# A retention kernel with its MLP: q only cast, the decay multiplied into the retention's result, and the work of all engines in another order

## The chip, the cores and the metric

One core of a Trainium2 chip runs the kernel. It has five engines with queues of their own: TensorE (PE, with PEld for its weight loads), VectorE (DVE), ScalarE (ACT), GpSimd (POOL) and SyncE (SP). Each engine takes its instructions in the order of the program and waits on semaphores where it needs another's result. Data move between the memory (HBM) and the core by DMAs that POOL, SP or ACT issue. The metric is the time of one execution in microseconds on the device; lower is better.

## The reference

Eight batches of eight heads, 576 positions, 64 wide; then a two-layer MLP over 4608 tokens:

```python
scores = scale * np.matmul(q, k.transpose(0, 1, 3, 2))
gamma = 1.0 - 2.0 ** (-5.0 - np.arange(H, dtype=np.float32))
rel = pos[:, None] - pos[None, :]
Dmat = np.where(rel >= 0, gamma[:, None, None] ** rel[None, :, :], 0.0)
attn_out = np.matmul(scores * Dmat[None, :, :, :], v)
x = np.ascontiguousarray(attn_out.transpose(0, 2, 1, 3)).reshape(B * S, H * D)
h = x @ w_in
return np.maximum(0.01 * h, h) @ w_out
```

The weight of a pair of positions is gamma to the power of their distance, so it splits into a factor of the later position (q's) and one of the earlier (v's).

## The kernel before

**Blocks.** The 4608 tokens are 36 blocks (`u`) of 128, each of two chunks of 64. A batch has nine chunks. Four blocks are a group `g` of 512 tokens, and there are nine groups. A position's decay is taken relative to the middle of a stretch of four chunks (256 positions), so that a table with one row for each position in the stretch serves all blocks.

**One block of retention.** `ld` loads q, k and v (0, 1, 2) as float32. `ck` casts k to float16. `cq` multiplies q with its decay and the scale and writes float16, `cv` does so for v; on DVE each is one multiplication with a broadcast table, on ACT eight small ones (`scaled`, L373). k and q are transposed, in blocks 0 to 7 on PE (`tp`, L411, with copies out of PSUM by `yt`, L418), later by a DMA of SP (`tr`, L397). `sa` makes the scores (L445), `mk` applies the causal mask (DVE, L460), `sb` makes the chunk's state (L454), `st` adds it to the running state (DVE, L485 to L491; at a stretch's end in two steps, through `stmp`, with gamma to the 256th), `sx` casts the state (L503, L506). `oa` makes the output from v and the masked scores and from q and the state (L542); from block 4 on it is parted into `ca` (scores of this block and the part of the output that crosses chunks) and `ow`. `x` (L591) casts the output from PSUM into the group's `xT`, float16, on ACT or DVE.

**The MLP.** Groups 0 and 1 run layer 1 as plain matmuls (`h`, L640, and the leaky ReLU `l`, L647). The other groups run it with seven products instead of eight (`a`, L833), and layer 2 does so for all groups (`b`, L911), with sums of weights and operands made by DVE (`ws`, `wm`, `xs`, `m`) and additions of the products (L857, L947). w_in comes in four quarters (`wi0` to `wi3`, L612), w_out in four (`wo`, L621), cast to float16 by POOL's DMAs.

**What sets the order.** `ORDER` is a list of job names, issued in that order: each engine's queue is the list with the other engines' jobs left out. `@n` picks a PSUM bank, and `+13@3` stands for 13 matmuls on a tile of zeros (`filler`, L977). `ENGINE` says which engine makes a cast or a copy. Pools have few buffers: a load for block `u + 4` waits until block `u`'s cast has read its buffer.

Of the kernel before, what the change touches and what calls it, by code (L numbers as in the profile page):

```python
# [33 lines left out]
class Plan:  # L34
# [52 lines left out]
    for eng, names in {  # L87
        "DVE": """
            ck0 cq0 sx0.0 yt0.0 cq1 sx0.1 cv1 cq2 sx1.0 yt2.1 ck3 cq3 yt3.1 cv3 sx2.1 yt3.0 cq4 cv4 x3 ck5 cq5
            cv5 yt5.1 cq6 sx5 cv6 cq7 ck7 cv7 yt7.0 b0.cA cv8 ck10 sx8.0 cv9 cq9 cq11 cq12 cv10 b1.cA cv13 ck15  # L90
            cv14 cq14 cv15 cq15 sx13.1 sx14 cq16 cv16 cv17 cq17 cq18 a2.3.k5 sx17.0 cv18 sx18 cq19 a3.1.u2 x17
            cv20 ck21 cq21 sx19 a3.2.k5 cq22 cv22 sx20 ck23 cv23 cq23 x20 cv24 cq25 sx23 a4.2.cA cv25 a4.2.u2
            cq26 cq27 cv27 sx25 a5.0.u2 a5.0.k5 cq28 cq29 cv29 ck30 cq30 cv30 ck31 cv31 cq32 sx30 cq33 ck33
            a6.0.cA cv33 cv34 ck34 cq35 cq34 a6.2.cA b5.u2 cv35 a6.3.u2 x32 a7.0.cA x33 a7.0.k5 b5.21 a7.1.cA
            b6.11 b6.u2 a7.3.cA a7.3.u2 a8.0.k5 b7.k5 a8.2.u2 a8.2.k5 b7.21 a8.3.u2 b8.21
        """,
        "ACT": """
            cv0 yt0.1 x0 ck1 ck2 yt1.1 yt1.0 cv2 yt2.0 x1 sx1.1 sx2.0 x2 sx3.0 ck4 sx3.1 yt4.1 yt4.0 ck6 sx4.1
            x4 yt5.0 x5 yt6.0 yt6.1 sx6 yt7.1 sx7 x7 x6 ck8 b0.11 cq8 ck9 b0.u2 cq10 b0.k5 cv11 ck12 sx9 x8 ck11
            cv12 sx10 cq13 b0.21 x9 ck13 sx11 b1.11 sx12 x10 b1.u2 x11 ck14 a2.0.cA b1.k5 a2.0.u2 a2.0.k5 x12  # L100
            a2.1.cA a2.1.u2 x13 a2.1.k5 ck16 ck17 sx15 a2.2.cA a2.2.u2 b1.21 a2.2.k5 sx16 x14 a2.3.cA x15
            a2.3.u2 ck18 b2.cA a3.0.cA b2.11 a3.0.u2 a3.0.k5 a3.1.cA cv19 b2.u2 x16 a3.1.k5 ck19 b2.k5 a3.2.cA
            ck20 cq20 a3.2.u2 cv21 b2.21 ck22 x18 a3.3.cA a3.3.u2 a3.3.k5 x19 b3.cA a4.0.cA b3.11 sx21 ck24
            a4.0.u2 a4.0.k5 cq24 a4.1.cA a4.1.u2 sx22.1 a4.1.k5 x21 b3.u2 ck25 b3.k5 ck26 sx24 a4.2.k5 x22 cv26
            a4.3.cA x23 a4.3.u2 a4.3.k5 ck27 b3.21 a5.0.cA b4.cA ck28 cv28 sx26.0 b4.11 x24 ck29 a5.1.cA a5.1.u2
            a5.1.k5 x25 sx27 sx28 b4.u2 a5.2.cA x26 sx29 b4.k5 a5.2.u2 a5.2.k5 x27 a5.3.cA ck32 a5.3.u2 cv32
            a5.3.k5 cq31 b4.21 x28 x29 sx31.1 a6.0.u2 a6.0.k5 sx32 b5.cA a6.1.cA b5.11 a6.1.u2 x30 a6.1.k5 x31
            a6.2.u2 a6.2.k5 sx33 b5.k5 ck35 a6.3.cA a6.3.k5 sx34 sx35.0 a7.0.u2 b6.cA a7.1.u2 a7.1.k5 a7.2.cA
            a7.2.u2 b6.k5 a7.2.k5 x34 x35 a7.3.k5 a8.0.cA b6.21 a8.0.u2 b7.cA b7.11 a8.1.cA b7.u2 a8.1.k5
            a8.1.u2 a8.2.cA a8.3.cA a8.3.k5 b8.cA b8.u2 b8.k5 b8.11x so8.11x b8.11y  # L110
# [11 lines left out]
    l0.4.256 tp4.0@2 x3 tp5.0@1 yt4.0 st3.1s ld6.1 h0.11.0@0 sx3.1 yt5.0 ld6.2 h0.9.0@2 yt4.1 ck5 cv4 ld7.0
    h0.10.0@1 l0.9.0 tp5.1@3 ld7.2 l0.10.0 ca4 sb4 h0.4.384@2 mk4 ld7.1 cv5 h0.8.0@1 l0.4.384 st4.1 ld8.2 yt5.1 ow4
    sb5 x4 h0.15.0@2 st5.0 sx4.1 st5.1 l0.11.0 h0.14.0@3 sx5 ld8.1 ca5 l0.14.0 cq6 l0.8.0 ld9.2 ws3.1 h0.13.0@0 mk5
    ld9.1 h0.0.128@3 l0.13.0 cv6 wo2 h0.0.384@1 l0.0.128 ld10.2 l0.15.0 tp6.0@0 h0.0.256@3 ck6 yt6.0 ld10.1 tp6.1@2
    l0.0.384 ow5 sb6 wo0 x5 h0.12.0@0 st6.0s yt6.1 ld8.0 h1.0.0@1 cv7 l0.0.256 cq7 ld9.0 h1.2.0@2 l1.0.0 ck7 st6.1
# [88 lines left out]
def kernel(  # L215
# [148 lines left out]
    def casts(u):  # L364
# [5 lines left out]
        def ck():  # L370
            copies[ke](out=by_half(t[:, 1]), in_=in_halves(t32[u, 1][:]))
# [680 lines left out]
```

## Time and profile before

| what | before |
|---|---|
| median of 3 runs (lowest, highest) | 279.20 us (279.14, 279.57) |
| the profiled execution: its time | 279.54 us |
| its span, first to last instruction | 277.7 us |
| PE busy | 268.1 us, 97% |
| PE's weight loads busy | 224.4 us, 81% |
| DVE busy | 229.8 us, 83% |
| ACT busy | 206.7 us, 74% |
| POOL busy | 72.4 us, 26% |
| HBM read, written | 36.81 MB, 9.44 MB |

Busy time is the time in which at least one instruction of the engine runs; matmuls overlap each other, and their ends are modelled. The profile gives for a group of instructions the number, the busy time, the mean duration of one, and the idle time ahead of them with what ended most of it. A timeline row has the start, the duration, engine, line, operation and the tiles (out `<-` in), how many were merged (`xN`), and idle time in brackets.

### The profile page before, as it was taken

What the parts mean: (1) busy time and instruction counts of PE and PEld (TensorE: products, weight loads), DVE (VectorE), ACT (ScalarE), POOL (GpSimd) and SP (SyncE); (2) the same over time, 40 slices, a digit from 0 to 9 for tenths busy, and PEclk for the clock granted to TensorE, in tenths of its full rate; (3) what the DMA queues carried; (4) which work ended last, traced back from release to release, by engine and by line L of the source; (5) the groups of instructions that cost most, each with busy time, mean ns of one, the idle gap of its engine ahead of it and who ended that gap; (6) DMA issues with size and microseconds to landing.
All of it is one profiled execution on the core that took longest, in us unless ns stands there. A gap on an engine that the chain in (4) does not pass through costs nothing.

```text
span 277.7 us, 10117 instructions
## 1 busy us (share of the span) xinstructions
PE 268.1 (97%) x4337; PEld 224.4 (81%) x4337; DVE 229.8 (83%) x431; ACT 206.7 (74%) x459; POOL 72.4 (26%) x92
## 2 busy tenths in 40 slices
...
GB/s 219 224 240 238 293 287 269 277 216 177 208 256 220 220 295 227 173 236 230 257 222 255 183 228 183 170 247 219 20 139 74 44 2 2 153 0 0 78 97 132
DMA packets 94364, 50.04 MB, mean 180 GB/s; under 512 B 83312, under 2 KB 88560, under 8 KB 94320
## 3 DMA queue, kind: packets, MB, share of 16 engines
...
q8 instruction: 34, 0.56, 0.8%
q10 hardware_dynamic: 432, 0.24, 0.3%
q14 instruction: 10, 0.08, 0.1%
HBM read 36.81 MB, written 9.44 MB: 167 GB/s over the span
## 4 chain that ended last, share of the span: by engine, by line
PE 91%; DMA 5%; POOL 1%; ACT 1%; issue 1%; DVE 1%; POOLq 0%
PE acc L911 39%; PE acc L833 32%; PE acc L640 10%; DMA t<-in_k_dram 5%; PE ot L542 5%; PE sc L454 2%; PE sc L445 2%; PE sc L911 1%; POOL t L346 1%; PE acc L411 1%; DVE s L487 0%; POOL w_in L612 0%; ACT st L503 0%; DVE qk L375 0%; DVE s L460 0%
## 5 line engine op out<-in xcount | busy, mean ns | idle before, releaser
L911 PEld LDWEIGHTS <-gt 128*128 128x128 f16 x720 | 69.8, 98 | 8.4
L346 POOL DMA_DIRECT2D t<-in_v_dram x40 | 34.2, 857 | 100.5 <-DVE v L375 64.0
L911 PE MATMUL acc<-w_out,gt 128*128 128x256 f16 x416 | 51.5, 273 | 0.0
L833 PEld LDWEIGHTS <-w_in 128*128 128x128 f16 x448 | 42.4, 98 | 5.6
L853 ACT ACTIVATE gt<-acc 128x512 f16<-128x512 f32 x56 | 33.4, 599 | 16.6 <-PE acc L833 16.4
L861 ACT ACTIVATE gt<-sum 128x512 f16<-128x512 f32 x56 | 34.8, 633 | 4.7 <-DVE sum L857 4.7
L911 PE MATMUL acc<-w_mix,gt 128*128 128x256 f16 x288 | 36.2, 273 | 0.0
L833 PEld LDWEIGHTS <-w_sum 128*128 128x128 f16 x336 | 32.2, 98 | 4.1
L833 PE MATMUL acc<-xs,w_sum 128*128 128x256 f16 x224 | 33.6, 273 | 0.0
L833 PE MATMUL acc<-xT,w_in 128*128 128x256 f16 x224 | 33.5, 273 | 0.0
L833 PE MATMUL acc<-xs,w_in 128*128 128x256 f16 x224 | 33.4, 273 | 0.0
...
L640 PE MATMUL acc<-xT,w_in 128*128 128x256 f16 (+2 forms) x272 | 30.8, 266 | 0.7 <-ACT qkT L418 0.4
L911 PEld LDWEIGHTS <-mix 128*128 128x128 f16 x288 | 28.1, 98 | 3.3
L460 DVE TENSOR_TENSOR s<-sc,cs 128x512 f16<-128x512 f32 x36 | 24.6, 684 | 4.4 <-PE sc L445 2.3
L640 PEld LDWEIGHTS <-w_in 128*128 128x128 f16 x272 | 22.0, 98 | 5.8 <-issue 0.9
L857 DVE TENSOR_TENSOR sum<-acc,k 128x512 f32<-128x512 f32 x28 | 19.2, 686 | 7.9 <-PE acc L833 5.7
L647 ACT ACTIVATE gt<-acc 128x512 f16<-128x512 f32 x32 | 18.2, 601 | 6.3 <-PE acc L640 6.2
L786 ACT COPY k<-acc 128x512 f32<-128x512 f32 x29 | 17.0, 588 | 7.5 <-PE acc L833 3.7
L375 DVE TENSOR_TENSOR qk<-t,cs 128x512 f16<-128x512 f32 x30 | 20.5, 684 | 2.3 <-DMA t<-in_q_dram 2.3
L591 ACT CAST xT<-ot 128x512 f16<-128x512 f32 x31 | 18.2, 588 | 4.6 <-PE ot L542 4.6
L381 ACT ACTIVATE v<-t,cs 128x64 f16<-128x64 f32 x72 | 18.3, 343 | 4.1 <-DMA t<-in_v_dram 3.4
...
## 6 DMA issues: line engine op xcount, KB each, us to landing
...
```

Of the source, the lines that this page charges most:

```text
L346: engine[eng].dma_start(out=t[CH * j : CH * j + rows], in_=(q, k, v)[x][b, :, CH * w : CH * w + rows, :].rearrange("h t d -> t h d"),)
L375: engine[e].tensor_tensor(out=view[0](out), in0=view[1](t32[u, 2 * x][:]), in1=view[1](decay(u, x)), op=MUL)
L381: nc.scalar.mul(out=out[:, at(h), :], in_=t32[u, 2 * x][:, h, :], mul=tab_sb[:, w, x, h : h + 1])
L460: landed[u] = nc.vector.tensor_tensor(out=s[:], in0=sc[:, :, 0], in1=mask_sb.unsqueeze(1).unsqueeze(1).to_broadcast([P, 2, NP, CH]), op=MUL,)
L591: moved[u] = copies[xe](out=x_of(u).rearrange("q c (j t) -> q j c t", j=2), in_=at)
L640: nc.tensor.matmul(out=a[:, n, :], lhsT=w_in16[:, c, (f0 + n) * P : (f0 + n + 1) * P], rhs=x[:, c, t0 : t0 + nt], start=(n == 0 and c == 0 ...
L647: nc.scalar.activation(out=y[:, f0 : f0 + nf, t0 : t0 + nt], in_=a[:], func=mybir.ActivationFunctionType.Lrelu)
L833: nc.tensor.matmul(out=r[:, f, :], lhsT=w[:, c, (2 * n + f) * P : (2 * n + f + 1) * P], rhs=rhs[:, c, :], start=fresh and c == 0 and f == ...
L853: w = op(what, "ACT", lambda: nc.scalar.activation(out=to(), in_=r[:], func=lr), after, [y], [r])
L857: what, "DVE", lambda: nc.vector.tensor_tensor(out=s[:], in0=r[:], in1=plus[:], op=ADD),
L861: f"l{g}.{n}.{what}", "ACT", lambda: nc.scalar.activation(out=to(), in_=s[:], func=lr), [j], [y],
L911: nc.tensor.matmul(out=(r[tb] if isinstance(r, tuple) else r)[:, tb, :], lhsT=lhs[n]()[:, f, tb * P : (tb + 1) * P], rhs=rhs[n][:, f, :], ...
```

## The change

- **q only cast.** `cq` no longer multiplies: it is a cast like `ck` (`plain`). The table of q's decays goes.
- **The decay goes into the result.** The factor of q's position is the same for all that one position's output sums, so it can be applied to the output: `x` is now a multiplication of the output in PSUM with a table `q_tab`, always on DVE. The table (four parts of 128x256, float32) is built on DVE at the start by four multiplications of two small tables (`tb0` to `tb3`). The constants that ACT's DMA brings grow from 148 to 236 columns.
- **The running state.** The two steps at a stretch's end work in place, without `stmp`; the float32 states get a pool of three buffers, apart from the float16 ones (four).
- **The zero tile** `idle` becomes a part of `w_mix`, which is written with its own contents later.
- **Order and engines.** `ENGINE` and `ORDER` are new throughout. Zero matmuls: 13 + 4 + 3 + 2 + 7 + 2 + 2 = 33 before, 9 + 6 + 2 + 1 + 2 + 2 + 4 + 3 + 3 + 1 + 5 = 38 now. PE now does blocks 0 to 3 whole before the first layer-1 group; before, three such groups and transposes of blocks 4 and 5 stood among them. On DVE there are 36 output multiplications (5 output casts before), no q multiplications (30 before), 24 casts of q and k (12 before) and 30 of v (27 before); on ACT 48 casts of q and k (24 before) and none of the outputs (31 before).

```diff
@@ ENGINE and ORDER, a line or two of each
-            ck0 cq0 sx0.0 yt0.0 cq1 sx0.1 cv1 cq2 sx1.0 yt2.1 ck3 cq3 yt3.1 cv3 sx2.1 yt3.0 cq4 cv4 x3 ck5 cq5
+            cv0 ck1 cv1 sx0.0 sx0.1 cv2 yt2.1 yt2.0 sx1.0 sx2.0 ck4 yt4.0 yt4.1 cv4 ck5 cv5 yt5.0 cv6 cv7 cv8 yt6.0
...
-    ld0.1 ld0.2 ld0.0 ld1.0 ld1.1 ld2.1 ck0 ld2.0 cq0 ld1.2 cv0 cq1 ld2.2 +13@3 tp1.0@0 wi1 tp0.0@1 tp0.1@2 sb0 +4@3
+    tb1 tb0 ld0.0 ld0.2 ld0.1 ld1.1 tb3 ld1.2 cq0 ck0 +9@3 tp0.0@3 tb2 ld1.0 yt0.0 +6@1 tp0.1@0 cv0 ld2.1 yt0.1 ck1
...
@@ tables
-    tab = np.zeros((P, len(kinds), 2, H))
+    tab = np.zeros((P, len(kinds), H))
...
-        tab[:, w, 0] = gamma[None, :] ** r * scale
-        tab[:, w, 1] = gamma[None, :] ** (-r)
+        tab[:, w] = gamma[None, :] ** (-r)
+    NB, FINE = BLK // CH, 16
+    fine, coarse = np.zeros((P, NP, FINE)), np.zeros((P, NP, BLK // FINE))
+    for c in range(NP):
+        for oo in range(2):
+            rows = slice(CH * oo, CH * oo + CH)
+            fine[rows, c] = gamma[2 * c + oo] ** np.arange(FINE)
+            coarse[rows, c] = gamma[2 * c + oo] ** (FINE * np.arange(BLK // FINE) - BLK / 2) * scale
...
-    idle = const_pool.tile([P, TOK], F16, name="idle")
+    idle = w_mix[:, 2, 0:2].rearrange("p f n -> p (f n)")
...
+    def q_table():
+        for a in range(NB):
+            def run(a=a):
+                nb = CH // FINE
+                nc.vector.tensor_tensor(
+                    out=q_tab[:, a].rearrange("p c (b r) -> p c b r", b=nb),
+                    in0=fine_sb.unsqueeze(2).to_broadcast([P, NP, nb, FINE]),
+                    in1=coarse_sb[:, :, a].unsqueeze(3).to_broadcast([P, NP, nb, FINE]), op=MUL,
+                )
+
+            steep.append(add(f"tb{a}", "DVE", run))
@@ casts
-        def cq():
-            scaled(t[:, 0], 0, qe, lambda h: 2 * (h % NP) + h // NP, (by_half, in_halves))
+        def plain(x, e):
+            copies[e](out=by_half(t[:, x]), in_=in_halves(t32[u, x][:]))
...
+        cast[u, 1] = add(f"ck{u}", ke, lambda: plain(1, ke), [loaded[u, 1]], [t], [t32[u, 1]])
+        cast[u, 0] = add(f"cq{u}", qe, lambda: plain(0, qe), [loaded[u, 0]], [t], [t32[u, 0]])
@@ running state
-        f, h = Buf(a_pool, [P, 2, NP, CH], FP, "s32", turn=u), Buf(a_pool, [P, 2, NP, CH], F16, "st16", turn=u)
+        f, h = Buf(f_pool, [P, 2, NP, CH], FP, "s32", turn=u), Buf(a_pool, [P, 2, NP, CH], F16, "st16", turn=u)
...
-                    tmp = t_pool.tile([P, NP, CH], FP, name="stmp")
-                    nc.vector.tensor_tensor(out=tmp, in0=x, in1=before[0][:, before[1]], op=ADD)
+                    nc.vector.tensor_tensor(out=to, in0=x, in1=before[0][:, before[1]], op=ADD)
                     nc.vector.tensor_tensor(
-                        out=to, in0=tmp, in1=gblk_sb.unsqueeze(2).to_broadcast([P, NP, CH]), op=MUL
+                        out=to, in0=to, in1=gblk_sb.unsqueeze(2).to_broadcast([P, NP, CH]), op=MUL
                     )
@@ output
-            moved[u] = copies[xe](out=x_of(u).rearrange("q c (j t) -> q j c t", j=2), in_=at)
+            moved[u] = nc.vector.tensor_tensor(
+                out=x_of(u).rearrange("q c (j t) -> q j c t", j=2), in0=at, in1=by_place, op=MUL
+            )
```

The queues at three places. First POOL's, from its first load on, before; `t_0`, `t_1` and `t_2` are the float32 tiles of q, k and v, and `x2` is a load in two halves of a block that spans two batches. The rows are v of block 0, q and k of block 1, k and q of block 2, v of blocks 1 and 2, a quarter of w_in, k and q of block 3, k of block 4, v of block 3:

```order
L346 DMA t_2_137<-in_v_dram 128x8x64
L346 DMA t_0_141<-in_q_dram 128x8x64
L346 DMA t_1_143<-in_k_dram 128x8x64
L346 DMA t_1_145<-in_k_dram 128x8x64
L346 DMA t_0_149<-in_q_dram 128x8x64
L346 DMA t_2_152<-in_v_dram 128x8x64
L346 DMA t_2_165<-in_v_dram 128x8x64
L612 DMA w_in_122<-in_moe_w_in_dram 128x4x512
L346 DMA t_1_220<-in_k_dram 128x8x64
L346 DMA t_0_226<-in_q_dram 128x8x64
L346 DMA t_1_260<-in_k_dram 64x8x64 x2
L346 DMA t_2_293<-in_v_dram 128x8x64
```

The same queue now: v of block 0, k, v and q of block 1, k, q and v of block 2, v, k and q of block 3, then the quarter of w_in and q of block 4:

```order
L362 DMA t_2_139<-in_v_dram 128x8x64
L362 DMA t_1_143<-in_k_dram 128x8x64
L362 DMA t_2_146<-in_v_dram 128x8x64
L362 DMA t_0_167<-in_q_dram 128x8x64
L362 DMA t_1_185<-in_k_dram 128x8x64
L362 DMA t_0_206<-in_q_dram 128x8x64
L362 DMA t_2_221<-in_v_dram 128x8x64
L362 DMA t_2_223<-in_v_dram 128x8x64
L362 DMA t_1_264<-in_k_dram 128x8x64
L362 DMA t_0_314<-in_q_dram 128x8x64
L640 DMA w_in_123<-in_moe_w_in_dram 128x4x512
L362 DMA t_0_326<-in_q_dram 64x8x64 x2
```

Block 3's three loads have moved ahead of the first quarter, which is the eleventh transfer now and was the eighth.

Second, DVE in the head, before, from the copy of block 2's transposed k on: block 3's k cast, states and masks of block 2, block 3's q, its transposes' copies, its v, block 4's q:

```order
L418 COPY qkT<-acc 128x512
L371 CAST qk_448<-t_1_220 128x2x4x64
L487 TENSOR_TENSOR s_451<-sc,s_329 128x256
L460 TENSOR_TENSOR s_458<-sc,cs 128x512
L487 TENSOR_TENSOR s_451<-sc,s_451 128x256
L375 TENSOR_TENSOR qk_448<-t_0_226,cs 128x2x4x64
L418 COPY qkT<-acc 128x512 x2
L375 TENSOR_TENSOR v_502<-t_2_293,cs 128x512
L375 TENSOR_TENSOR qk_476<-t_0_326,cs 128x2x4x64
```

And now, at the same place, from the copies of block 2's transposes on: mask of block 1, states of block 2, then outputs of blocks 0, 1, 3 and 2 (`xT`) between states and masks:

```order
L440 COPY qkT<-acc 128x512 x2
L482 TENSOR_TENSOR s_388<-sc,cs 128x512
L527 CAST st_383<-s_268 128x256
L509 TENSOR_TENSOR s_412<-sc,s_268 128x256
L509 TENSOR_TENSOR s_412<-sc,s_412 128x256
L527 CAST st_450<-s_412 128x256
L617 TENSOR_TENSOR xT<-ot,q_tab 128x2x4x64
L509 TENSOR_TENSOR s_485<-sc,s_412 128x256
L482 TENSOR_TENSOR s_487<-sc,cs 128x512
L617 TENSOR_TENSOR xT<-ot,q_tab 128x2x4x64
L482 TENSOR_TENSOR s_554<-sc,cs 128x512
L617 TENSOR_TENSOR xT<-ot,q_tab 128x2x4x64 x2
```

Block 3's casts have left DVE for ACT, and the outputs stand on DVE.

Third, DVE where the sums of w_out's quarters (`w_mix`) begin, before:

```order
L460 TENSOR_TENSOR s_1236<-sc,cs 128x512
L686 TENSOR_TENSOR w_mix<-w_out_123 128x1024
L887 TENSOR_TENSOR gt<-gt 128x4x256
L686 TENSOR_TENSOR w_out_123<-w_out_123 128x4x256
L375 TENSOR_TENSOR v_1306<-t_2_895,cs 128x512
L686 TENSOR_TENSOR w_mix<-w_out_123 128x1024
```

And now, with the outputs of blocks 6 and 7 ahead of them and the casts of q of blocks 8 and 9 among them:

```order
L617 TENSOR_TENSOR xT<-ot,q_tab 128x2x4x64
L482 TENSOR_TENSOR s_1216<-sc,cs 128x512
L511 TENSOR_TENSOR s_1246<-sc,s_1118 128x256
L512 TENSOR_TENSOR s_1246<-s_1246,cs 128x256
L617 TENSOR_TENSOR xT<-ot,q_tab 128x2x4x64
L915 TENSOR_TENSOR gt<-gt 128x4x256
L401 CAST qk_1158<-t_0_1093 128x2x4x64
L714 TENSOR_TENSOR w_mix<-w_out_124 128x1024
L401 CAST qk_1242<-t_0_1102 128x2x4x64
```

The multiplication of a v has left this place, and two outputs and two casts of q stand there that were on ACT or further back.

More of the change, by code (lines that the diff above doesn't have):

```diff
@@ L65 @@
     ap=4,
+    fp=3,
     cp=5,
@@ L100 @@
[L100 to L109, printed above, removed]
@@ L122 @@
[L122 to L126, printed above, removed]
@@ L137 @@
-    ld15.1 m1.0.1 ow10 b0.11 ca11 m1.2.0 a2.0.p1.0@2 b1.11 so0.0 b1.p5.0@0 m1.1.1 a2.0.cA@1 cv13 x10 b1.p5.1 mk11
-    sx12 ld17.2 b1.p6.1 m1.2.1 m1.3.0 ow11 b1.u2 sb13 ca12 m1.3.1 a2.0.p2.0 x11 b1.p7.0 tr13 ld15.0 a2.0.11 xs2.0
-    cq14 b1.k5 ld16.0 a2.0.p5.0@2 st13.1 b1.p7.1 a2.0.k5 xs2.1 ld17.0 mk12 a2.0.p6.0 xs2.2 b1.p3.0 a2.0.u2 sx13.1
-    ck15 ck14 ld16.1 xs2.3 a2.0.p7.0 a2.0.p3.0 a2.0.22 b1.p3.1 a2.0.12 l2.0.22 a2.0.p4.0 b1.22 l2.0.12 a2.1.p1.0@2
-    cv14 a2.0.21 b1.p4.0 b1.12 ld18.2 a2.1.p5.0@1 cq15 sb14 a2.1.k5 ow12 ca13 tr14 a2.1.cA@0 b1.p4.1 st14.0 x12
@@ new lines @@
+    m1.3.1 x11 xs2.0 xs2.1 a2.0.11 ck15 cv14 ck14 xs2.3 mk12 xs2.2 ld17.2 cq14 a2.0.p5.0@2 tr13 a2.0.k5 a2.0.p6.0
+    cv15 st13.1 ld15.0 b1.p7.1 ld16.0 a2.0.p3.0 a2.0.u2 b1.p3.1 ld17.0 a2.0.12 a2.0.p7.0 a2.1.p1.0@2 l2.0.12 b1.12
+    sb14 ow12 a2.0.22 b1.22 a2.1.cA@0 l2.0.22 ca13 a2.0.p4.0 a2.1.p2.0 a2.0.21 cq16 ld16.1 ld18.2 cq15 a2.1.p6.0
+    cq17 cv16 a2.1.11 st14.0 a2.1.u2 st14.1 a2.1.p5.0@1 x12 b1.p4.0 b1.p4.1 a2.1.k5 ws4.1 sx14 sx13.1 tr14 tr15
+    b1.21 ld17.1 mk13 ld19.2 a2.1.p3.0 a2.1.p7.0 ck16 a2.2.p1.0@3 tr16 ow13 a2.1.22 ld18.0 a2.2.cA@2 sb15 a2.1.12
@@ new lines @@
+    xs6.3 a6.1.p5.0@3 m5.1.0 a6.0.p4.0 cv32 b5.11 ld35.0 a6.1.p1.0@1 st31.1 ow29 cv34 m5.1.1 sb32 ca30 b5.p6.0 mk30
+    a6.0.21 a6.1.cA@0 a6.1.k5 a6.1.p6.0 a6.1.p3.0 a6.1.u2 a6.1.p2.0 x29 a6.1.11 l6.0.22 a6.1.p7.0 a6.1.22 tr33 ow30
+    ca31 a6.2.p1.0@1 a6.1.p4.0 b5.p6.1 a6.1.21 a6.1.12 st32.0 l6.1.12 b5.p5.0@3 st32.1 sx31.1 a6.2.cA@0 a6.2.p2.0
+    sx32 b5.u2 a6.2.11 cv33 tr34 mk31 a6.2.p6.0 b5.p5.1 x30 a6.2.p5.0@1 a6.2.u2 sb33 b5.k5 a6.2.k5 m5.3.1 ow31 ca32
+    m5.3.0 l6.1.22 st33.0s ld35.1 st33.1 a6.2.p7.0 a6.2.22 a6.2.p3.0 a6.2.12 x31 b5.p3.0 b5.p3.1 a6.2.p4.0
@@ L211 @@
+    b8.u2 m8.3.0 b8.p7.0 m8.3.1 b8.p7.1 b8.p3.0 b8.11x b8.p3.1 b8.22 b8.12 so8.11x b8.p4.0 b8.p4.1 b8.p2.1 so8.22
+    so8.12 b8.11y b8.21 so8.21 so8.11y
 """
@@ L368, in casts, with cv @@
         ke, qe, ve = by(f"ck{u}", "ACT"), by(f"cq{u}", "DVE"), by(f"cv{u}", "DVE")
-        def ck():
-            copies[ke](out=by_half(t[:, 1]), in_=in_halves(t32[u, 1][:]))
-        def scaled(out, x, e, at, view):
-            if e != "ACT":
-                engine[e].tensor_tensor(
-                    out=view[0](out), in0=view[1](t32[u, 2 * x][:]), in1=view[1](decay(u, x)), op=MUL
-                )
+        def plain(x, e):
+            copies[e](out=by_half(t[:, x]), in_=in_halves(t32[u, x][:]))
+        def cv():
+            if ve != "ACT":
+                engine[ve].tensor_tensor(out=s[:], in0=t32[u, 2][:], in1=decay(u), op=MUL)
                 return
```

225 lines of the change are left out of this document (120 added, 105 removed), and 12 rows, old and new, of the table loads.

## The prediction

> **What bounds the kernel now.** I read the busy time in stages first, then PE's waits, then PE's instructions in order of time, and last the groups of DVE and ACT. The columns of the stages are microseconds, busy time and instructions of PE, PEld, DVE, ACT and POOL, the granted clock, DMA share and GB/s.
>
> ```profile
> 14.00:21.00 7.00, 5.40 (x98) 3.16 (x95) 4.58 (x11) 3.03 (x7) 3.65 (x5) 1.00 0.96 237
> 21.00:28.00 7.00, 6.14 (x139) 4.04 (x139) 5.14 (x11) 4.44 (x9) 6.55 (x9) 1.00 1.15 239
> 28.00:40.00 12.00, 12.00 (x239) 8.74 (x237) 7.90 (x16) 8.85 (x17) 9.44 (x12) 1.00 1.10 293
> 60.00:100.00 40.00, 40.00 (x763) 34.30 (x761) 37.20 (x72) 34.34 (x83) 8.38 (x10) 1.00 1.03 227
> 100.00:140.00 40.00, 40.00 (x739) 34.60 (x737) 38.34 (x75) 37.34 (x91) 8.02 (x10) 1.00 1.08 229
> ```
>
> From 28 us on PE is busy all the time, so nothing after that point can shorten the run unless PE gets less work, and the change removes no real matmul. Only the first 28 us have PE time to win: waits, and matmuls on zeros. The same rows show the danger: DVE is busy 93 to 96% of the middle of the run, ACT 86 to 93%. PE's two longest items of waiting, each with its sum, how often and the longest, are these:
>
> ```profile
> PE acc L411 <- DVE qk L375: 2.2, 2, 2.0
> PE acc L411 <- DVE qk L371: 1.3, 1, 1.3
> ```
>
> They make 3.5 us, all in the head: the transposes (L411) of the first blocks wait for their casts. PE's own rows (start, duration, what, in brackets the idle time before):
>
> ```profile
> 1.23 4.35 PE L980 MATMUL acc<-idle 128*128 128x512 f16 x13 [1.23 <-DVE idle L316]
> 7.61 0.84 PE L411 MATMUL acc<-ident,qk 128*128 128x128 f16 x12 [2.03 <-DVE qk L375]
> 8.38 0.32 PE L454 MATMUL sc<-v,qk 64*64 64x64 f16 x16
> 8.63 1.04 PE L980 MATMUL acc<-idle 128*128 128x512 f16 x4
> ...
> 12.80 0.32 PE L542 MATMUL ot<-s,v 64*64 64x64 f16 x16
> 12.95 0.56 PE L542 MATMUL ot<-qkT,st 64*64 64x64 f16 x8
> 13.45 1.69 PE L980 MATMUL acc<-idle 128*128 128x512 f16 x7
> 15.06 0.32 PE L445 MATMUL sc<-qkT 64*64 64x64 f16 x16
> ...
> 18.20 1.04 PE L640 MATMUL acc<-xT,w_in 128*128 128x256 f16 x8
> 19.08 0.59 PE L980 MATMUL acc<-idle 128*128 128x512 f16 x2
> ...
> 22.60 1.05 PE L640 MATMUL acc<-xT,w_in 128*128 128x128 f16 x16 [0.24 <-ACT xT L591]
> 23.58 0.32 PE L542 MATMUL ot<-s,v 64*64 64x64 f16 x16
> ...
> 25.30 2.75 PE L640 MATMUL acc<-xT,w_in 128*128 128x512 f16 x12 [0.41 <-ACT qkT L418]
> ```
>
> The brackets add 0.24 and 0.41 us in which layer 1 (L640) waits for a finished block and a copied transpose: 4.1 us of waiting in all. The reader sees two things more. PE runs without a gap from 25.30 us. And by then it has done more than blocks 0 to 3: three layer-1 groups (8, 8 and 16 matmuls, 0.88 us from 18.20 to 19.08, 0.98 us from 22.60 to 23.58, so 2.8 us for the three) and three sets of four transposes for blocks 4 and 5 (the x12 row goes from 7.61 to 8.38, so 0.25 us a set). Had it done blocks 0 to 3 alone, the same state would have come at 25.30 - 2.8 - 0.75 = **21.75 us**. That is the number to compare, because the new order does just that: blocks 0 to 3 whole, then layer 1.
>
> **The change part by part: the head.** In the new order PE issues 9 zero matmuls, then 29 in small lots, the 8 sets of transposes, scores, states and outputs of blocks 0 to 3, and then its first layer-1 group. The prices: a set of transposes 0.25 us; a block's states 0.25 us (8.38 to 8.63) and its scores the same; a block's output 0.65 us (12.80 to 13.45); a zero matmul 0.23 us (seven from 13.45 to 15.06). The first ones are slower:
>
> ```profile
> L980 PE MATMUL acc<-idle x7: 524/634/634, 1.2 to 3.8; 128*128 128x512 f16 x7
> ```
>
> Seven of them start between 1.2 and 3.8 us, 0.43 us apart, though the granted clock is printed as 1.00. So the first nine take 7 x 0.43 + 2 x 0.23 = 3.4 us. The sum: 1.2 (start) + 3.4 + 29 x 0.23 = 6.7, + 8 x 0.25 + 8 x 0.25 + 4 x 0.65 = 6.6, gives 17.9 us. The same prices for the kernel before give 1.2 + 4.35 + 20 x 0.23 = 4.6, + 6.6 + 2.8 + 0.75 = 20.3, and with its waits of 4.1 us 24.4, where 25.30 was measured: small gaps of 0.9 us, of which I take 0.8 for the new head. So it is 18.7 us with no wait, and 22.8 with as much waiting as now. Which of the two is nearer is read from what the transposes wait for:
>
> ```profile
> 6.86 0.69 DVE L375 TENSOR_TENSOR qk<-t,cs 128x512 f16<-128x512 f32 x1 [0.71 <-DMA t<-in_q_dram]
> 17.23 0.68 DVE L371 CAST qk<-t 128x512 f16<-128x512 f32 x1 [2.23 <-DMA t<-in_k_dram]
> 11.56 2.03 ACT L381 ACTIVATE v<-t,cs 128x64 f16<-128x64 f32 x8 [0.47 <-DMA t<-in_v_dram]
> ```
>
> The long waits came from block 3. Its k is POOL's ninth transfer, behind a quarter of w_in, and its cast began only at 17.23 us. The second POOL transfer was there at 6.86, the seventh at 11.56: 0.94 us each. In the new order block 3 is transfers eight to ten, all ahead of w_in, so it is there by 11.56 + 3 x 0.94 = 14.4 us, and PE asks for it at about 15, after 29 of the zero matmuls and most of blocks 0 to 2. That wait goes. What is late next: the states of block 0 wait for v's cast (v lands at 6.1, 0.69 on DVE; PE is there at 6.5): 0.35 us. Block 1's k wait 0.2, and block 1's and block 3's scores wait for copies of transposes on ACT, which has an eight-part cast of 2.03 us (block 3's v) ahead of them: 0.45. Together **1.0 us**, so the first layer-1 group starts at 18.7 + 1.0 = 19.7 us. Against 21.75 that is **2.05 us won**; the ends are 3.05 (no wait) and 1.05 lost (as much waiting as now).
>
> The first w_in quarter goes from eighth to eleventh place. In the chain of waits block 3's k, right behind it, took 8.90 us from issue:
>
> ```profile
> 8.31 8.90 DMA t<-in_k_dram
> L612 POOL DMA_DIRECT2D w_in<-in_moe_w_in_dram x4: 767/770/780, 7.6 to 22.9; - x4
> DMA to landing us min/median/max: 6.8/7.8/9.2
> ```
>
> It landed at 17.21, so quarter and k together took at most 17.21 - 11.56 = 5.65 us. Behind 14.4 us the quarter lands at latest at 19.3 (5.65 less one load of 0.76 to 0.94): ahead of 19.7, hidden by the zero matmuls, with 0.4 us to spare. The last quarter was issued at 22.9 and landed by 32.1. In the new order the same bytes are ahead of it, and PE needs it after 12 layer-1 groups of 0.88, four sets of transposes and about four pieces of attention of 0.25, at 19.7 + 12.6 = 32.3: hidden, but with no slack. I take 0.1 us, ends 0 and 1.5 (if DMA starts as much later as the first quarter's wait would be).
>
> **The change part by part: DVE and ACT.** The edits on q and on the outputs shift work between these groups:
>
> ```profile
> L375 DVE TENSOR_TENSOR qk<-t,cs 128x512 f16<-128x512 f32 x30 | 20.5, 684 | 2.3 <-DMA t<-in_q_dram 2.3
> L591 ACT CAST xT<-ot 128x512 f16<-128x512 f32 x31 | 18.2, 588 | 4.6 <-PE ot L542 4.6
> L381 ACT ACTIVATE qk<-t,cs 128x64 f16<-128x64 f32 x48 | 12.2, 345 | 0.0
> L460 DVE TENSOR_TENSOR s<-sc,cs 128x512 f16<-128x512 f32 x36 | 24.6, 684 | 4.4 <-PE sc L445 2.3 <-PE sc L454 2.0
> ```
>
> DVE loses 30 multiplications of 684 ns (20.5 us) and gets 12 more casts of some 0.42 (5.0; one is quoted below) and 31 more outputs: the trace has no such multiplication, but L460 has its form (PSUM times a float32 table, float16 out), 684 ns, so 21.2 us. With the four small tables (a 128x256 instruction is 0.42, so 1.7 us, at 4 to 6 us, when DVE waits for data) DVE is some 7 us fuller (- 20.5 + 5.0 + 21.2 + 1.7) over the run. ACT loses 18.2 and 12.2 us and gets 24 casts. Off the critical path by the totals, but not evenly. I counted DVE's instructions between two points of PE, the first product of group 0's layer 2 (49.24 us) and the first of group 3's layer 1 (101.36). Back to back they start closer than they last:
>
> ```profile
> 49.23 0.69 DVE L887 TENSOR_TENSOR gt<-gt 128x1024 f16<-128x1024 f16 x1
> 49.83 0.69 DVE L686 TENSOR_TENSOR w_out<-w_out 128x1024 f16<-128x1024 f16 x1
> 53.30 0.41 DVE L485 COPY s<-sc 128x256 f32<-128x256 f32 x1
> 53.63 0.41 DVE L371 CAST qk<-t 128x512 f16<-128x512 f32 x1
> ```
>
> A long one takes 0.60 us of the queue, a short one 0.33, a block end in two dependent halves 0.8. Before: 64 long, 19 short, 3 ends and 2 casts of 0.2 are 47.5 us in 52.1 us of PE, 91%. After: 60 long, 23 short, 4 ends are 47.0, and PE has six layer-1 groups and a piece of attention less there (they now stand ahead of it), 52.1 - 5.5 = 46.6 us: **101%**. What is queued behind a late DVE instruction is nearly everything PE asks for: masks, states, outputs of attention, mixes of w_out, sums of layer 1. Bounds: 0.4 us (47.0 - 46.6) if it runs as closely as in 49.23 to 53.63; 7.5 us if none of the 83 overlaps its neighbour (0.085 us each, 7.1, more). Below 0.4 it could be nothing, as the many jobs between have some slack. I take 0.5, nearest to the quoted rows, which show the overlap kept. The state buffers cut from four to three hold a block that was read two blocks earlier: nothing. The tail keeps PE's order of the last products: nothing.
>
> The head's pace: the slow stretch of seven lasts 2.8 us, from 1.2 to 4.0. If nine zero matmuls with a wait behind them were too few to end it and it lasted as long again, work of 2.8 x 0.23 / 0.43 = 1.5 us would take 2.8: 1.3 us lost. That the stretch ended before the ninth started speaks against it; I take nothing. [...]
>
> **The sum.** The profiled execution took 279.54 us (span 277.7 and 1.84 around it). 279.54 - 2.05 + 0.1 + 0.5 = 278.1. The median of the runs is 279.20, 0.34 lower; so I predict **277.7 us** for the median.
>
> **The rivals.**
> - *DVE becomes the bound* (slower). Place: the stage from group 0's layer 2 to group 3's. For it: 101% there, and masks and outputs now on one in-order engine. Against it: between 100 and 140 us DVE was 96% busy and PE waited for nothing. Price: 0.085 us for each of 83 instructions that starts without overlap; from 20 of them on (1.7 us) the gain is gone. With 50 of 83 the time is 277.7 + 4.2 - 0.5 = 281.4. Chance 0.15.
> - *The head's waits only move* (moving the loads changes nothing). If PE waits 4.1 us as now, at casts on ACT or at the first quarter, layer 1 starts at 22.8 and the time is 279.2 + 1.05 + 0.6 = 280.8. For it: ACT's 2.03 us cast and five more zero matmuls. Against it: block 3's data come 3 us earlier. Chance 0.08.
> - *Half of each* (no change): waits of 2.5 us and DVE 0.6 us give 279.2 - 0.55 + 0.7 = 279.3. A second slow stretch of PE belongs here: 277.7 + 1.3 = 279.0. [...]
>
> **How the numbers follow.** My forecast has 0.62, with its own range of 276.2 (no wait in the head, no DVE cost) to 278.6 (below the 0.2%, about 0.6 us, that a measurement of this kernel can tell from no change). Same 0.15, slower 0.23. The range of 8 in 10 runs from 276.2 to 280.8: it leaves out the greater part of the DVE case and a little below.
>
> **What would show it.** Right: PE's first layer-1 row near 19.7 us with four outputs of attention ahead of it, no wait over 0.5 us of the transposes for casts, PE without gaps to the end. Wrong in the head: a wait for DMA at block 3's casts, or of L668 (the new line of layer 1) for w_in. Wrong on DVE: waits of PE for DVE between 50 and 100 us, and DVE above 97% busy there with PE below 100%.

## The result, and the profile after

The changed kernel takes **302.56 us** (median of 4 runs, 300.12 to 312.12) against 279.17 (278.87 to 279.57) for the kernel before on the same chip: 1.081 times the time, 95% interval 1.070 to 1.091 (here and below, disturbed executions are left out of the ratios but not of the medians, so differences between runs are taken from the ratios). The prediction, 277.7 us in a range of 276.2 to 280.8, has the wrong sign. The profiled execution of the changed kernel took 304.47 us, its span 302.7.

The stages of the changed kernel, in the columns of the prediction (us, busy time and instructions of PE, PEld, DVE, ACT and POOL, granted clock, DMA share, GB/s):

```profile
5.00:10.00 5.00, 3.48 (x53) 1.79 (x51) 3.50 (x9) 2.27 (x4) 5.00 (x6) 1.00 1.03 216
14.00:21.00 7.00, 5.17 (x142) 2.96 (x141) 4.43 (x11) 4.19 (x14) 2.94 (x5) 0.97 1.15 218
21.00:28.00 7.00, 6.55 (x96) 3.51 (x95) 4.37 (x8) 1.62 (x4) 5.01 (x6) 0.52 1.19 234
60.00:100.00 40.00, 32.96 (x512) 27.80 (x510) 29.70 (x57) 18.96 (x49) 5.05 (x7) 0.87 1.09 194
100.00:140.00 40.00, 38.31 (x738) 32.67 (x737) 37.10 (x73) 34.01 (x69) 8.77 (x11) 1.00 1.13 201
```

The first row is the one to stop at. In the kernel before the same stretch reads:

```profile
5.00:10.00 5.00, 2.91 (x39) 1.56 (x37) 2.62 (x5) 3.53 (x12) 5.00 (x6) 1.00 1.00 323
```

Both kernels load practically nothing but 256 KB pieces of q, k and v there, both have the DMA engines busy all the time (share 1.0), and the one moves 323 GB/s, the other 216. In the records of the DMA packets, a packet of 4096 bytes in POOL's queue lasts 195 ns before (median, 5 to 12 us) and 309 now. So the loads themselves became slower. PE's longest waits (in total, how often, longest) and its start of layer 1:

```profile
PE ot L563 <- DMA qkT<-qk: 7.0, 1, 7.0
PE acc L861 <- DVE sum L885: 3.1, 1, 3.1
PE sc L476 <- issue: 2.4, 2, 1.5
```

```profile
24.24 2.31 PE L1008 MATMUL acc<-w_mix 128*128 128x512 f16 x5
26.35 3.83 PE L668 MATMUL acc<-xT,w_in 128*128 128x256 f16 x35
...
63.13 0.32 PE L476 MATMUL sc<-v,qk 64*64 64x64 f16 x16
70.50 0.32 PE L563 MATMUL ot<-qkT,st 64*64 64x64 f16 x6 [7.04 <-DMA qkT<-qk]
```

Layer 1 starts at 26.35 us (19.7 was forecast). The five zero matmuls ahead of it take 2.31 us, where 1.1 would be full pace (they start 0.22 us apart at 5.1 to 6.2 us): the clock is at 0.52 there. At 63 us PE waits 7.0 us for block 8's transpose, the first that a DMA makes. In the chain of waits the eighth load of POOL and this transpose look so (start, duration):

```profile
7.55 7.91 DMA t<-in_v_dram
...
56.03 14.42 DMA qkT<-qk
```

Two things to explain, then: slow loads from the first microsecond on, and a transpose that takes 14.4 us (3.6 in the kernel before).

### The profile page after: what moved, and what is told of

Read it like the earlier page. It is cut to its first block, busy times and chain, and to the rows that moved or that the text cites. A ratio compares the mean times of both kernels' runs of the same rounds, so it can differ in the third digit from the quotient of the medians.

```text
span 302.7 us, 10053 instructions
## 1 busy us (share of the span) xinstructions
PE 277.7 (92%) x4342; PEld 229.3 (76%) x4342; DVE 235.9 (78%) x450; ACT 188.8 (62%) x381; POOL 72.2 (24%) x92
## 4 chain that ended last, share of the span: by engine, by line
PE 72%; DMA 15%; SPq 4%; ACT 3%; POOL 2%; issue 2%; DVE 1%; ACTq 0%; DVEq 0%; POOLq 0%
PE acc L939 31%; PE acc L861 23%; PE acc L668 9%; DMA t<-in_k_dram 8%; DMA qkT<-qk 5%; SPq L362 4%; PE ot L563 3%; DMA t<-in_v_dram 3%; POOL t L362 2%; PE sc L476 2%; PE sc L467 1%; PE sc L939 1%; PE acc L1008 1%; PE acc L433 1%; ACT v L409 1%
## 5 line engine op out<-in xcount | busy, mean ns | idle before, releaser
L861 PEld LDWEIGHTS <-w_in 128*128 128x128 f16 x448 | 43.0, 98 | 10.2 <-issue 4.5
L889 ACT ACTIVATE gt<-sum 128x512 f16<-128x512 f32 x56 | 33.9, 630 | 7.7 <-DVE sum L885 7.7
L401 ACT CAST qk<-t 128x512 f16<-128x512 f32 x48 | 29.2, 622 | 10.4 <-DMA t<-in_k_dram 6.7
L668 PE MATMUL acc<-xT,w_in 128*128 128x256 f16 (+2 forms) x272 | 32.2, 275 | 1.1 <-issue 1.1
L939 PEld LDWEIGHTS <-mix 128*128 128x128 f16 x288 | 29.2, 102 | 4.6
L668 PEld LDWEIGHTS <-w_in 128*128 128x128 f16 x272 | 23.0, 101 | 7.2 <-issue 1.9
L811 ACT COPY u<-acc 128x512 f32<-128x512 f32 x35 | 20.5, 585 | 12.4 <-PE acc L939 6.7
L617 DVE TENSOR_TENSOR xT<-ot,q_tab 128x512 f16<-128x512 f32 x36 | 24.3, 683 | 3.9 <-PE ot L563 3.9
L509 DVE TENSOR_TENSOR s<-sc,s 128x256 f32<-128x256 f32 x40 | 16.8, 420 | 10.4 <-PE sc L467 7.3
L800 ACT COPY acc<-acc 128x512 f32<-128x512 f32 x30 | 17.2, 574 | 10.0 <-DVE sum L885 5.5
```

The source lines that it names most:

```text
L401: copies[e](out=by_half(t[:, x]), in_=in_halves(t32[u, x][:]))
L617: moved[u] = nc.vector.tensor_tensor(out=x_of(u).rearrange("q c (j t) -> q j c t", j=2), in0=at, in1=by_place, op=MUL)
L668: nc.tensor.matmul(out=a[:, n, :], lhsT=w_in16[:, c, (f0 + n) * P : (f0 + n + 1) * P], rhs=x[:, c, t0 : t0 + nt], start=(n == 0 and c == 0 ...
L800: copies[ce](out=B[:], in_=A[:])
L811: op("u2", ue, lambda: copies[ue](out=u2[:], in_=B[:]), [done["6"]], [u2], [B])
L861: nc.tensor.matmul(out=r[:, f, :], lhsT=w[:, c, (2 * n + f) * P : (2 * n + f + 1) * P], rhs=rhs[:, c, :], start=fresh and c == 0 and f == ...
```

## The experiments

What could slow a load whose shape, source and queue are the same? Its destination. The constants grew and a table was added, and the pools lie behind them: the built program puts the float32 tiles of the loads at byte 75776 of each partition before, a multiple of 512, and at 79200 now, 32 past a multiple of 64 and 96 past one of 256. **Theory A** is that offset; **rival B** is the order.

**1. 32 unused bytes.** `const_pool.tile([P, n], FP, name="pad")` behind the constants, n = 8:

```diff
     warm = const_pool.tile([P, 1], FP, name="warm")
+    const_pool.tile([P, 8], FP, name="pad")
```

> The changed kernel with 32 unused bytes per partition behind the constants and nothing else: every tile of the pools moves by 32 bytes, so that the float32 tiles of the loads begin at byte 79232 (a multiple of 64) and not at 79200 (32 past one). Theory A, the offset: the loads are slow because their tiles begin 32 bytes past a multiple of 64. Then a 4096-byte DMA packet takes about 195 to 200 ns again (309 in the changed kernel), a load of the head 0.76 us (1.20), the first layer-1 product starts at 19 to 22 us (26.35), the stall of 7.2 us at 63 us goes, and the time is 276 to 281 us. Rival B, the order: the new order itself, with the constants larger and block 8's transpose asked for earlier, makes the waits. Then packets stay near 300 ns or the waits stay without them, and the time stays at 295 us or more. Between 283 and 293 both have a part.

Measured: 303.9 us, ratio 1.064 (1.058 to 1.070), 216 GB/s from 5 to 10 us, packets at 309 ns. By itself a point for B; for A it says that a multiple of 64 is not enough.

**2. 160 unused bytes** (n = 40).

> The changed kernel with 160 unused bytes per partition in the same place: the tiles of the loads begin at 79360, a multiple of 512 as in the kernel before. Theory A with 64 bytes as what counts: the same time as with 32 bytes of padding, within 0.3%. Theory A with a larger step (128, 256 or 512): faster than that, with packets at 195 ns where 32 bytes of padding gives a value between 195 and 309. Rival B: 295 us or more here too.

Measured: **286.65 us**, ratio 1.027 (1.021 to 1.032), packets at 195 ns again. The stretch from 5 to 10 us, and the chain and PE's rows at the places of above:

```profile
5.00:10.00 5.00, 4.83 (x79) 2.75 (x79) 4.13 (x10) 3.64 (x7) 5.00 (x6) 1.00 1.02 330
```

```profile
7.71 4.52 DMA t<-in_v_dram
...
47.36 13.75 DMA qkT<-qk
```

```profile
18.55 1.25 PE L1009 MATMUL acc<-w_mix 128*128 128x512 f16 x5
19.64 3.70 PE L669 MATMUL acc<-xT,w_in 128*128 128x256 f16 x48
...
54.45 0.32 PE L477 MATMUL sc<-v,qk 64*64 64x64 f16 x16
61.15 0.32 PE L564 MATMUL ot<-qkT,st 64*64 64x64 f16 x6 [6.39 <-DMA qkT<-qk]
```

Not one instruction differs between 1 and 2, only addresses. By the ratios, 10 us go with them from run 1 (1.064 to 1.027) and 15 from the changed kernel (1.081); why those two lie 5 us apart, with packets equally slow, is not shown. Layer 1 starts at 19.64 us. What stays, 7 us above the kernel before, is another cause: the transpose is as slow as ever.

**3. The kernel before, moved by 32 bytes.** The other direction, order and arithmetic untouched.

> The kernel before, its order and arithmetic untouched, with 32 unused bytes behind its constants: the tiles of the loads begin at 75808 (32 past a multiple of 64) and not at 75776. Theory A: packets of 4096 bytes take about 309 ns (195 before), loads of the head 1.2 us, block 3's k lands at 22 us or later (17.2), and the time rises to 288 to 305 us. Rival B: 279 us, within 0.3%.

Measured: 298.19 us, ratio 1.065 (1.060 to 1.070), packets at 309 ns, 220 GB/s from 5 to 10 us. The offset alone costs the old order 18 us, no less than the new one.

**4. Three offsets in one kernel.** In the kernel before, k, v and q get pools of their own with pads between.

> The kernel before with its k tiles at a multiple of 512, its v tiles at 64 past one and its q tiles at 96 past one (32 past a multiple of 64), all others as they were. This measures the disputed cost by itself, in one run. Theory A with 64 bytes: from 28 us on k and v loads land as far apart as before (0.76 us for 256 KB), a q load costs about 0.4 us more. Theory A with 128 bytes or more: v is slow as well. If the step between loads is 0.76 us for all three, the offset of the tile isn't what made the loads slow.

Measured: 287.86 us, ratio 1.029 (1.023 to 1.035), 264 GB/s from 5 to 10 us, between the two rates. In the landings of the first loads, v and q come 1.0 to 1.2 us after the load ahead of them, k of blocks 1 and 2 0.6 to 0.8. So 64 past a multiple of 512 (v) is slow too.

**5. 416 unused bytes** (n = 104), a multiple of 256 that is none of 512.

> The changed kernel with 416 unused bytes: the tiles of the loads begin at 79616, a multiple of 256 but not of 512. It measures the step of the offset: with 256 as the step, packets of 4096 bytes take 195 ns and the time is that of the 160-byte padding, 285.5 to 289 us; with 512, packets take about 309 ns and the time is 297 us or more.

Measured: 287.64 us, ratio 1.028 (1.022 to 1.033), packets at 195 ns, 334 GB/s. The step is 256 bytes: run 1 lay 128 past such a multiple and was slow.

**6. The loads' tiles alone** at a multiple of 512, all others 32 past a multiple of 64.

> The changed kernel with only the float32 tiles of the loads moved to a multiple of 512; the tiles that transposes write and stores read, and all tiles that only engines touch, stay 32 bytes past a multiple of 64. If the loads alone made the loss, the time is that of the kernel with all tiles moved, 285.5 to 289 us, with packets of 4096 bytes at 195 ns. If transposes, stores or the engines are slowed by the offset too, it lies between that and 302, at 291 us or more.

Measured: 288.55 us, ratio 1.030 (1.024 to 1.037), 323 GB/s. The intervals of 2, 5 and 6 overlap: as far as these runs can tell, the loads alone made this part of the loss. The stores' packets last 168 ns there, 159 in the kernel before.

So theory A stands with 256 bytes as its step; why the offset slows the packets stays open. Now the 7 us that stay. **Theory C**: the transpose of block 8 crawls since it is issued into a backlog of loads. **Rival D**: taking the wait away only shows the next one. The edits from here on are made to the kernel of 2.

**7. Block 8's crossing part later.**

```diff
-    ... b0.cA@3 ca8 h1.4.256@1 ...
+    ... b0.cA@3 h1.4.256@1 ...
-    mk8 b0.k5 b0.p7.1 b0.p3.0 tr9 ... ow8 sb11 ca9 ... tr10 b0.p4.1 b0.21
+    b0.k5 b0.p7.1 ca8 mk8 b0.p3.0 tr9 ... ow8 sb11 ... tr10 b0.p4.1 ca9 b0.21
```

> The changed kernel with its tiles at multiples of 512 (160 unused bytes) and one part of the order taken back: PE's crossing part of block 8 (ca8, which reads block 8's transpose) stands seven products of group 0's layer 2 and a layer-1 group later, 7.0 us of PE, and ca9 3 us later. Theory C: with the offset mended one wait is left, 6.4 us of ca8 for block 8's transpose, which lands at 61.1 us because its 256-byte packets are served a few at a time as long as the loads of POOL fill the DMA engines; behind it PE runs at half clock for 6.8 us (3.4 us of work lost). Then both go: no wait over 1 us, and 285.6 - 6.4 - 3.4 = 275.8, so 275.5 to 278 us. Rival D: the transpose only hides the next late thing (DVE, or the next transposes and q loads of SP), and PE waits elsewhere: 281 us or more.

Measured: 284.94 us, ratio 1.017 (1.012 to 1.022): a miss. The 6.4 us wait is gone, and PE waits for DVE instead, and DVE for two DMAs:

```profile
PE acc L940 <- DVE w_out L715: 2.9, 1, 2.9
PE sc L468 <- DVE s L512: 1.4, 1, 1.4
```

```profile
DVE qk L402 <- DMA t<-in_k_dram: 3.9, 1, 3.9
DVE w_mix L715 <- DMA w_out<-in_moe_w_out_dram: 3.6, 1, 3.6
```

The last quarter of w_out, which the sums of layer 2's weights need, landed at 58.25 us; k of block 12 stood on SP's queue behind a load whose issue was held for 10 us. Rival D is right, and C is sharpened by it: the transpose is slow because the DMA engines are full. In the trace's packets the loads and w_out fill them, but for single microseconds, beyond 60 us in 2 and 7. In the kernel before their share falls to 0.76 and 0.57 from 56 to 58 us, as its first transpose is issued. In 2, 45 to 130 packets of 256 bytes get through in a microsecond while loads run (51 to 58 us), and about 1000 behind them.

**8. The same edit with the offset kept.**

> The changed kernel with its tiles where they were (32 past a multiple of 64) and the later place of ca8 and ca9 alone. Theory C: the 7.2 us wait at 63 us goes and with it most of the 10.2 us of half clock behind it, while the slow loads stay: about 302.6 - 7 - 4 = 291.5, so 288 to 295 us. If the slow loads bound the stage in any case, it stays at 299 us or more.

Measured: 303.63 us, ratio 1.064 (1.058 to 1.071): by the ratio 5 us below the changed kernel, the same as run 1, where 11 were forecast; with slow loads the later place doesn't pay as forecast.

**9. Zero matmuls in the wait.** `+26@1` ahead of `ca8` in the kernel of 2.

> The changed kernel with its tiles at multiples of 512, and 26 zero matmuls (5.6 us at full pace) put ahead of ca8, where PE waits 6.4 us for block 8's transpose. No wait is taken away. Theory C says that 3.4 us of what that wait costs is the half clock behind it: with PE busy in the wait no half-clock stretch comes, and the time is 286.65 - 3.4 = 283.3, so 282.5 to 284 us. If the half clock costs nothing by itself (later slack makes up for it), the time stays at 286 to 287.

Measured: 287.6 us, ratio 1.025 (1.020 to 1.029): no difference from 2, where 3.4 us less was forecast. A wait of 2.7 us stayed behind the zero matmuls, and a half-clock stretch of 3.4 us (before: 6.8) behind it. What the half clock costs by itself is not shown.

**10. Less to load.** The kernel of 7, with two quarters of w_out set to zero by POOL and not loaded: it leaves out half of w_out in layer 2.

> The kernel with 160 unused bytes and the later ca8, with two of w_out's four quarters not loaded but set to zero on POOL, which leaves out half of w_out in layer 2. It takes about 6 us of DMA out of the first 60 us and changes nothing else. Theory C (the backlog bounds): the wait for w_out goes, the transpose of block 8 lands 5 to 6 us earlier (about 58 us), SP's queue comes free as much earlier, and the time falls by 3 to 6 us, to 279 to 282. If the transposes or SP's queue are slow for a reason of their own, block 8's still lands at 61 us or later and the time falls by less than 3 us.

Measured: 284.77 us, ratio 1.014 (1.009 to 1.020). The transpose landed at 57.2 us (63.9 in 7), 4.8 after its issue, and SP's load behind it was issued in 0.45 us; that is theory C's forecast for the DMA side, although the transpose was also issued 4.7 us later than in 7. The time hardly fell (3 to 6 us were forecast). PE has a new wait of 2.7 us at 41 us (its row `PE ot L564 <- DVE st L525`): a cast of DVE took 3.27 us while POOL set the first quarter to zero. Whether the zeroing did that is not shown: the cast began 1.1 us ahead of it, and nothing of DVE was stretched beside the second. For the time the run tells nothing.

**11. w_out first, the transpose late.** In the kernel of 7:

```diff
-    ... wo0 ld8.0 ... ld9.0 ... ld10.0 ... wo1 ... ld11.2 ... wo3
+    ... wo0 ld8.0 ... wo1 wo3 ld9.0 ld10.0 ... ld11.2
-    ck10 cq8 ... cv10 cq9 ... tr8 ... cq10 ... cv11 sb10 ... l1.4.256
+    ck10 ... cv10 ... sb10 ... l1.4.256 cq8 tr8 cq10 cv11 cq9
```

> The kernel with 160 unused bytes and the later ca8, and two more edits in the order: w_out's last two quarters go ahead of the loads of q9, q10 and v11 on POOL, and block 8's q cast, and with it block 8's transpose, is asked for at about 54 us, not 47. Theory C, sharpened: what bounds PE at 55 to 67 us is the DMA engines, which hold a backlog of loads until 58 to 61 us in every kernel here; a transpose issued into that backlog crawls, delays w_out's last quarter (58.25 us instead of 55.9) and blocks SP's queue for 10 us. Then w_out's last quarter lands by 53 us, the 2.9 us wait for it goes, the transpose lands within 5 us of its issue, and the 1.4 us wait at 67 us and the half clock of 3.4 us go: 284.9 - 2.9 - 1.4 - 1.7 = 278.9, so 277.5 to 281 us. Rival D: other work is late next (the casts of blocks 9 to 11, now later on DVE and ACT): 283 us or more.

Measured: **282.28 us**, ratio 1.009 (1.006 to 1.013). This is above C's 277.5 to 281 and below D's 283. Block 8's transpose was issued at 57.5 us and landed 2.8 later, the next one took 6.4:

```profile
DMA to landing us min/median/max: 2.8/4.6/6.4
```

The wait for w_out is gone. One wait in the middle stays, 2.6 us of PE for the state of DVE (L512), and behind DVE's queue stands this:

```profile
DVE qk L402 <- DMA t<-in_k_dram: 3.6, 1, 3.6
```

It is `ck12`, which the new `ENGINE` has on DVE (ACT before); DVE takes its work in order, and sums and states stand behind a cast whose load isn't there.

**12. ck12 later** (behind `x8`).

> The kernel with 160 unused bytes, the later ca8, w_out first and the late transpose, and one more part of the new assignment moved: DVE's cast of k12 stands behind block 8's output instead of ahead of the state that ends block 10's stretch. Theory C: one wait is left in the middle, 2.6 us at 62.4 us, since DVE (in order) waits 3.6 us for k12, a load that stands behind block 8's transpose on SP, and the state behind it holds a PSUM bank; PE then runs at half clock for 3.4 us. Then both go: 282.28 - 2.6 - 1.7 = 278.0, so 277 to 279.5 us, below the kernel before (279.6). That is my forecast for the change with its loads and its transposes in place. Rival D: yet another late thing takes its place: 281 us or more.

Measured: **281.72 us** (280.80 to 286.50), ratio 1.007 (1.004 to 1.011). C's 277 to 279.5 us did not come; D's number did. The profiled execution took 280.80, with no stretch of half clock between 6.4 us and the last matmuls. The wait went, smaller ones came at 83 to 97 us:

```profile
PE acc L862 <- DVE sum L886: 0.9, 1, 0.9
PE sc L477 <- issue: 0.8, 1, 0.8
PE acc L862 <- DVE xs L842: 0.6, 1, 0.6
```

**13. ck15 later too.**

> The kernel of the last repair (tiles at multiples of 512, ca8, w_out, block 8's transpose and ck12 moved) with DVE's cast of k15 later too: it stood ahead of sums and states while its load, behind two transposes on SP, landed at 81.7 us, and DVE, in order, waited 1.8 us for it; PE waited 0.6 and 0.9 us for DVE's sums behind it at 83 to 85 us. Theory C: these 1.5 us go, 280.8 - 1.5 = 279.3, so 278 to 280 us. Rival E (DVE itself is the bound from 80 to 100 us, with the outputs now on it): the waits only move, and it stays at 280.5 us or more.

Measured: 285.01 us (281.24 to 287.16), ratio 1.010 (1.001 to 1.020). DVE no longer waited there, and PE's waits moved to ACT's copies (1.5 and 0.8 us, at 77 and 90 us). The time cannot be told from run 12's. The waits only move, as rival E says, but not for its reason: they went to ACT, and DVE was busy for 34.6 of the 40 us from 60 to 100.

**14. The arithmetic alone**, in the order and on the engines of the kernel before.

> The change's arithmetic alone in the order and the assignment of the kernel before (tiles at multiples of 512): q cast, the table built, the outputs multiplied on DVE, the state in place, three state buffers. DVE gets 31 outputs of 0.60 us of its queue, loses 30 x 0.27 and gets the tables, some 12 us in all, ACT loses 18 us. If DVE's load is what matters (the rival of the prediction, from 20 late instructions on), PE waits for DVE between 100 and 140 us, where DVE was busy 96% already, and the time is 281 to 288 us. If DVE's queue has slack, it is within 1 us of the kernel before: 279 to 280.5.

Measured: 286.74 us, ratio 1.025 (1.022 to 1.028), in the range forecast for a DVE whose load matters. With outputs on DVE the old order loses 7 us. The profiled execution took 291.97 us, so only the kind of its waits is read. PE's longest wait there, 4.3 us at 168 us, is for a DMA transpose. Apart from that PE waits for DVE in many small pieces, of which these are some:

```profile
PE acc L435 <- DVE qk L403: 1.9, 2, 1.2
PE acc L670 <- DVE xT L619: 1.0, 3, 0.3
PE ot L565 <- DVE s L484: 0.9, 2, 0.6
PE acc L863 <- DVE xs L843: 0.8, 1, 0.8
```

No version of the change beat the kernel before; run 12 comes nearest, 0.4 to 1.1% above it.

## Why the prediction was wrong

**The head.** The step that failed first is the price of a load: "The second POOL transfer was there at 6.86, the seventh at 11.56: 0.94 us each. In the new order block 3 is transfers eight to ten, all ahead of w_in, so it is there by 11.56 + 3 x 0.94 = 14.4 us". The count of transfers was right, the 0.94 us was carried from a kernel whose tiles lay at multiples of 512 to one where they don't. With the tiles back in place (2) block 3's last load lands at 14.38 us and layer 1 starts at **19.64** (forecast 14.4 and 19.7); the first w_in quarter lands at 18.9 ("at latest at 19.3") and the last at 31.0, without a wait of PE. PE idles for 1.06 us on the way, where 1.8 were forecast (waits of 1.0, small gaps of 0.8), so part of the agreement is luck: other terms were 0.7 us too small. Still the head's mechanism was right and its size came out, and the larger part of the loss came from an effect that no row of the trace before could show: I read the new table and the larger constants as four short instructions on DVE, and not as bytes that move all that lies behind them.

The price of the offset is a measured one: 309 ns a packet for 195, 58% more (runs 1 and 2), with a step of 256 bytes by runs 1, 2 and 5. What makes it, no run shows.

**From the head's gain to the end.** "Against 21.75 that is 2.05 us won": the step took what the head wins as won at the end. It failed too, apart from the offset. An estimate, from PE's real matmuls weighted by their spacing in the trace: run 2 is 2.2 us ahead of the kernel before at 28 us and 2.8 at 52, but 6 behind from 72 us to the end. That PE is busy from 28 us on doesn't say how little slack its data have. In the kernel before, DVE's first use of w_out's last quarter, the issue of block 8's transpose on SP and PE's first use of it are these rows:

```profile
56.70 0.68 DVE L686 TENSOR_TENSOR w_mix<-w_out 128x1024 f16<-128x1024 f16 x1
```

```profile
56.36 1.33 SPq L397 DMA_TRANSPOSE qkT<-qk  x1
```

```profile
61.72 0.23 PE L542 MATMUL ot<-qkT,st 64*64 64x64 f16 x8
```

The quarter landed at 55.91 us and the transpose at 59.95. The DMA engines are full until 56 us (a share of 1.07 to 1.21 in each microsecond from 50 to 56), so by these rows PE could win some 0.8 us before it met w_out and 1.8 before it met the transpose, and the new order put the transpose's use 7 us earlier (54.8 us in the kernel of 2). I looked at POOL's loads and at DVE, and never at SP's transposes. In the kernel of 2 it cost 6.4 us of wait and 6.8 us at half clock, of which the first 2 lie in the wait:

```profile
59.00:66.00 7.00, 4.85 (x45) 3.55 (x45) 3.85 (x9) 0.60 (x1) 0.00 (x0) 0.51 1.05 211
```

Runs 7, 11 and 12 take it down to 2 us above the kernel before, by taking parts of the order back.

**DVE.** "I take 0.5" for a stage loaded to 101%. Between 100 and 140 us of the kernel of 2:

```profile
100.00:140.00 40.00, 39.89 (x690) 34.48 (x688) 38.87 (x78) 34.99 (x71) 8.90 (x11) 1.00 1.09 231
```

DVE is 97% busy (38.87 of 40), and PE loses 0.1 us: there the load costs nothing. The stage that the 101% speaks of, from group 0's layer 2 to group 3's layer 1, takes 50.4 us in run 12 (46.6 was forecast): PE is busy for 47.7 of them, DVE for 45.7, with 88 instructions (87 forecast). So 0.5 was too small, PE loses 2.7 there, but DVE is not full. PE's waits for DVE come from order: a cast that waits for a late load holds all that stands behind it (runs 7 and 11). The rival "DVE becomes the bound" priced overlap that is lost, and with DVE idle for 4.7 of the 50.4 us that is not what run 12 shows. With the old order (14) the extra outputs do cost 7 us; how much of that is DVE's load and how much the place of the outputs in its queue, no run separates. In the prediction's sum for this stage, 60 long, 23 short and 4 ends make 46.8 us by its prices, not 47.0.

**The second slow stretch**, taken as nothing. With the nine zero matmuls the slow start ended at 4.2 us in the changed kernel and at 4.5 in run 2. In the profiles of runs 6, 9, 10, 11 and 12, with the same nine, it lasted to 6.4 to 6.7 us, though the clock is printed as 1.00 there (in run 12 zero matmuls still take 634 ns at 4.6 us, against 380 at full pace). So the stretch that was priced at 1.3 us does come in some executions; but layer 1 starts at 20.14 to 20.32 us in them and at 19.64 to 20.08 in runs 2, 5, 7 and 13, so it costs some tenths of a microsecond. What brings it in some executions, no run shows. The changed kernel's later half clock, at 11 to 14 us, 21 to 28, around the 7 us wait (0.74 from 60 to 80 us) and at 158 to 161, is another matter: it came behind waits, the first two times behind waits of 0.6 to 1.5 us.

**The rest.** No wait was traced to the three state buffers, and from 180 to 260 us PE is busy all the time in runs 2, 11 and 12. In sum: the head's 2.1 us was right, 10 to 15 us came from the offset and 7 from transposes and w_out behind a full DMA; with both mended 2 us remain. They are lost between 66 and 100 us, where the waits move from DVE to ACT when one is taken away; this is run 12, which by the estimate above is still 2.2 us ahead at 64 us:

```profile
60.00:100.00 40.00, 37.28 (x715) 31.16 (x713) 36.00 (x70) 26.79 (x59) 8.03 (x11) 1.00 1.16 235
```

Which single edit of the new order they hang on is open.
